# Causal score quarters and a redistributed mask in a gated linear attention kernel with a router

## The chip, the cores and the metric

The kernel runs on one core of one Trainium2 chip. Its time is the device time in microseconds (us) of one execution; the time before is 432.96 us, the median of 3 runs (432.19 to 433.65). The engines are called as in the profile: PE is TensorE (PEld its weight loads), DVE is VectorE, ACT is ScalarE, POOL is GpSimd, SP is SyncE, which only issues transfers. SBUF is the working memory, PSUM the memory that PE writes, in banks of 512 float32 values per partition. All data is float32.

## The reference, cut to what matters

A gated linear attention feeds a mixture of eight experts. For each of 4 batches and 8 heads a state of 48 x 48 decays and grows along 768 time steps; the result is regrouped to 3072 tokens of 384 values, a router picks one expert for each token, and that expert's two layers are run.

```python
# attention, q k v alpha: (4, 8, 768, 48)
for t in range(S):
    state = alpha[:, :, t, :, None] * state + np.einsum('bhd,bhe->bhde', k[:, :, t], v[:, :, t])
    y[:, :, t] = np.einsum('bhd,bhde->bhe', q[:, :, t], state)
# router and experts, x: (3072, 384), E = 8, F = 1024
logits = xn @ en.T / tau            # xn, en: rows over their norms
expert_idx = np.argmax(logits, axis=1)
for e in range(E):
    mask = expert_idx == e
    h = np.maximum(x[mask] @ w1[e], 0.0)
    out[mask] = gate_w[mask, None] * (h @ w2[e])
```

## The kernel before

The sequence of a batch is cut into 6 chunks of 128 steps, so there are NS = 24 chunks, each with 8 heads in NP = 4 pairs; a pair's two heads (hh = 0, 1) lie in partitions 0 to 63 and 64 to 127, 48 of each 64 used. A loop of 27 steps works as a pipeline: step s loads and decays chunk s, forms the scores of chunk s-1, and mixes chunk s-2 into rows. Within a chunk, the output of time i is a sum over times j up to i, so scores above the diagonal are masked.

Decays and scores. `pa`, `pk`, `pq` and `pkb` are transposes by PE into PSUM; they and `px` take turns in three banks.

```python
def decays(s):
    pa = turned(at_s[i], "pa")                      # PE, 4 transposes
    nc.vector.tensor_tensor_scan(r..., pa..., inr...)
    pk = turned(kt_s[i], "pk")
    nc.vector.tensor_tensor(krf, pk, r, ALU.mult)
    pq = turned(qt_s[i], "pq")
    nc.scalar.copy(qc, pq)
def decay_queries(s):
    nc.vector.reciprocal(ini..., rv[:, :, 0:1])
    d["a_scan"] = nc.vector.tensor_tensor_scan(a, pa, ini, 0.0, ALU.mult, ALU.add)
    nc.gpsimd.tensor_tensor(qs, d["qc"], a, ALU.mult)
# keys_back(s): pkb = transposes of kr, nc.scalar.copy(kb, pkb)
def scores(s):
    d["sm"] = sm = [work.tile([P, NP, P], FP32, name=f"sm{hh}") for hh in range(2)]
    sc = [ps_sc.tile([P, NP, P], FP32, name=f"sc{hh}") for hh in range(2)]   # a bank each
    for p in range(NP):
        for hh in range(2):
            sl = slice(DP * hh, DP * hh + DP)
            mm(sc[hh][:, p], lhsT=kr[sl, p], rhs=qs[sl, p], start=True, stop=True)
    nc.vector.tensor_tensor(sm[0], sc[0], causal.to_broadcast([P, NP, P]), ALU.mult)
    nc.scalar.copy(sm[1], sc[1])
    nc.gpsimd.affine_select(out=sm[1], in_=sm[1], pattern=[[0, NP], [1, P]], base=0,
        channel_multiplier=-1, compare_op=ALU.is_ge, fill=0.0)
```

Mixing, rows and routing. `px` holds a chunk's rows and, in 8 further columns per quarter, its logits.

```python
def mix_chunk(s):                     # after mix_states, which adds dec x qs to pyx
    for hh in range(2):
        ... mm(pyx[hh]..., lhsT=vt[:, 2 * p + hh], rhs=sm[hh][:, p], ...)
        nc.scalar.copy(yT[hh]..., pyx[hh][:, 0:YX])          # ycols
def update(s): ...                    # pd = kb x v, then state on DVE
def rows(s):
    ... mm(px[sl, hh, q], lhsT=yT[hh][:, q, sl], rhs=sel[:, hh, q], ...)
    nc.vector.tensor_reduce(x[:, LG : LG + E]..., px[:, :, :, 2 * D :]..., op=ALU.add)
    nc.scalar.copy(x[:, 0:DM]..., px[:, :, :, 0 : 2 * D]...)
def choose(g):                        # DVE: top, win, win, best, chosen; POOL: before
def place(g, total=False):            # PE: rk, two products; DVE:
    nc.vector.tensor_tensor(at, rk, ch, ALU.mult)
    nc.vector.tensor_reduce(row.unsqueeze(2), at, axis=AX.X, op=ALU.add)
    nc.vector.tensor_copy(dest[:, s0:s1], row)
    send.extend(range(s0, s1))
for s in range(NS + 3):
    load(s + 2); keys_back(s - 1); decays(s); decay_queries(s); decay_state(s - 1)
    scores(s - 1)                     # issued after the scan a of step s
    mix_states(s - 2); mix_chunk(s - 2); update(s - 1); rows(s - 2)
    r = s - 3                         # a group whose last row is r is placed here
    ...
    # one placed row is scattered to its expert per step; after row 15: fetch_early(), weights(0)
    # a group whose last row is s - 2 is chosen here
```

The expert phase follows the loop; the change does not touch it.

Of the kernel before, what the change touches and what calls it, by code (L numbers as in the profile page):

```python
# [9 lines left out]
FP32 = mybir.dt.float32  # L10
I32 = mybir.dt.int32
AF = mybir.ActivationFunctionType
ALU = mybir.AluOpType
AX = mybir.AxisListType
# [13 lines left out]
def kernel(  # L28
# [12 lines left out]
    nc = tc.nc  # L41
    B, H, S, D = q.shape
    E, DM = expert_emb.shape
    F = w1.shape[2]
    P = 128
    DP = 64
    NP = H // 2
    NCH = S // P
    N = B * S
    NS = N // P  # L50
# [4 lines left out]
    HALF = P // 2  # L55
# [3 lines left out]
    LG, TK, ROW = DM, DM + E, DM + E + 1  # L59

    GROUPS = (
        (0, 3), (3, 6), (6, 9), (9, 12), (12, 14), (14, 16), (16, 19), (19, 21), (21, 23), (23, 24)
    )
    GMAX = max(b - a for a, b in GROUPS)

    S0, EARLY = 16, 2
# [12 lines left out]
    causal = consts.tile([P, 1, P], FP32)  # L79
# [19 lines left out]
    dest = consts.tile([P, NS], I32)  # L99
# [90 lines left out]
    def mm(*args, **kwargs):  # L190
        last["pe"] = nc.tensor.matmul(*args, **kwargs)  # L191
# [4 lines left out]
    def in_turn():  # L196
        return tc.issue_after(last["pe"].ins) if last else ExitStack()


    with ExitStack() as c1:  # L200
        keep = c1.enter_context(tc.tile_pool(name="keep", bufs=1))
        work = c1.enter_context(tc.tile_pool(name="work", bufs=2))
# [9 lines left out]
        kt_s = [keep.tile([P, H, DP], FP32, name=f"kt{i}") for i in range(NBUF)]  # L212
        vt_s = [keep.tile([P, H, DP], FP32, name=f"vt{i}") for i in range(NBV)]

        NR = 3
        r_s = [keep.tile([P, NP * P], FP32, name=f"r{i}") for i in range(NR)]

# [3 lines left out]
        def fixed_parts():  # L221
            for i in range(NBUF):
                nc.gpsimd.memset(at_s[i][:, :, D:DP], 1.0)

                nc.gpsimd.memset(at_s[i][0:1], 0.0)
                nc.vector.memset(kt_s[i][:, :, D:DP], 0.0)
                nc.vector.memset(qt_s[i][:, :, D:DP], 0.0)
                if i == 0:
                    nc.gpsimd.memset(inr, 0.0)
                    for p in range(NP - 1):  # L230
                        nc.gpsimd.memset(inr[:, p * P + P - 1 : (p + 1) * P], 1.0)
                    for j in range(NR):
                        nc.vector.memset(r_s[j][:, NP * P - 1 :], 1.0)
                if i < 2:
                    nc.vector.memset(ini_s[i], 0.0)
            make_upper_triangular(nc, causal[:, 0], val=1.0, diag=True)
            for i in range(NBV):
                nc.vector.memset(vt_s[i][:, :, D:DP], 0.0)

# [104 lines left out]
        def place(g, total=False):  # L344

            s0, s1 = GROUPS[g]
            n = s1 - s0
            ch = chosen[:, s0:s1]
            bank = ps_mm.tile([P, GMAX + 1, E], FP32, tag="mm", name="rk")
            rk = bank[:, 0:n]  # L350
            rkf = rk.rearrange("p s e -> p (s e)")
            mm(
                rkf, lhsT=ones, rhs=before[:, s0:s1].rearrange("p s e -> p (s e)"),
                start=True, stop=False,
            )
            mm(
                rkf, lhsT=earlier, rhs=ch.rearrange("p s e -> p (s e)"),
                start=False, stop=True,
            )
            if total:  # L360

                mm(bank[:, GMAX], lhsT=ones, rhs=before[:, s1], start=True, stop=True)
            at = work.tile([P, GMAX, E], FP32, name="at_row")[:, 0:n]
            nc.vector.tensor_tensor(at, rk, ch, ALU.mult)
            row = work.tile([P, GMAX], FP32, name="row")[:, 0:n]
            nc.vector.tensor_reduce(row.unsqueeze(2), at, axis=AX.X, op=ALU.add)
            nc.vector.tensor_copy(dest[:, s0:s1], row)
            send.extend(range(s0, s1))
            if not total:
                return None  # L370
            m = work.tile([P, E], FP32, name="n")
            nc.vector.tensor_tensor(m, bank[:, GMAX], ebase, ALU.subtract)
            return m

        def first_expert(n):

            ok = work.tile([P, E], FP32, name="ok")
            nc.vector.scalar_tensor_tensor(
                out=ok, in0=n, scalar=float(EARLY * P), in1=first, op0=ALU.is_ge, op1=ALU.mult
            )  # L380
            lead = work.tile([P, 1], FP32, name="lead")
            nc.vector.tensor_reduce(lead, ok, axis=AX.X, op=ALU.max)
            nc.vector.tensor_scalar(lead, lead, -1.0, float(E), ALU.mult, ALU.add)
            nc.vector.tensor_scalar(turn_f, cols, lead, None, ALU.add)
            wrap = work.tile([P, E], FP32, name="wrap")
            nc.vector.tensor_scalar(wrap, turn_f, float(E), float(E), ALU.is_ge, ALU.mult)
            nc.vector.tensor_tensor(turn_f, turn_f, wrap, ALU.subtract)
            nc.vector.tensor_copy(turn_i, turn_f[0:1])
            r0 = work.tile([1, E], FP32, name="r0")
            nc.vector.tensor_scalar(r0, turn_f[0:1], float(N), None, ALU.mult)  # L390
            nc.vector.tensor_scalar(r0[:, 0:1], r0[:, 0:1], float(EARLY * P), None, ALU.add)
            nc.vector.tensor_copy(row0, r0)
# [67 lines left out]
        def behind(s):  # L460

            queue = ExitStack()
            for call in st[s]["last"]:
                queue.enter_context(tc.issue_after(call.ins))
            return queue
# [94 lines left out]
        def scores(s):  # L560

            d = st[s]
            kr, qs = d["kr"], d["qs"]
            d["sm"] = sm = [work.tile([P, NP, P], FP32, name=f"sm{hh}") for hh in range(2)]
            sc = [ps_sc.tile([P, NP, P], FP32, name=f"sc{hh}") for hh in range(2)]
            for p in range(NP):
                for hh in range(2):
                    sl = slice(DP * hh, DP * hh + DP)
                    mm(
                        sc[hh][:, p], lhsT=kr[sl, p], rhs=qs[sl, p], start=True, stop=True  # L570
                    )
            nc.vector.tensor_tensor(sm[0], sc[0], causal.to_broadcast([P, NP, P]), ALU.mult)
            nc.scalar.copy(sm[1], sc[1])
            nc.gpsimd.affine_select(
                out=sm[1], in_=sm[1], pattern=[[0, NP], [1, P]], base=0,
                channel_multiplier=-1, compare_op=ALU.is_ge, fill=0.0,
            )

        NQ = NP // 2
# [33 lines left out]
        def rows(s):  # L615

            yT = st[s]["yT"]
            px = ps_tr.tile([P, 2, NQ, 2 * D + E], FP32, tag="tr", name="px")
            for hh in range(2):
                for q in range(NQ):  # L620

                    for i in range(2):
                        sl = slice(i * HALF, (i + 1) * HALF)
                        mm(
                            px[sl, hh, q], lhsT=yT[hh][:, q, sl], rhs=sel[:, hh, q],
                            start=True, stop=True, skip_group_check=True,
                        )
            g = group_of[s]
            s0, s1 = GROUPS[g]
            if s == s0:  # L630
                x_g[g] = work.tile([P, GMAX, ROW], FP32, name="x", bufs=4)[:, 0 : s1 - s0]
            x = x_g[g][:, s - s0]
            nc.vector.tensor_reduce(
                x[:, LG : LG + E].unsqueeze(2), px[:, :, :, 2 * D :].rearrange("t a q e -> t e a q"),
                axis=AX.XY, op=ALU.add,
            )
            nc.scalar.copy(
                x[:, 0:DM].rearrange("t (q j a d) -> t a q j d", q=NQ, j=2, a=2),
                px[:, :, :, 0 : 2 * D].rearrange("t a q (j d) -> t a q j d", j=2),
            )  # L640


# [21 lines left out]
        def warm(n):  # L664

            pw = ps_mm.tile([P, P], FP32, tag="mm", name="pw")
            for _ in range(n):
                mm(pw, lhsT=ident, rhs=ident, start=True, stop=True)

        send = []  # L670
        warm(7)
        fixed_parts()
        load(0)
# [3 lines left out]
        for s in range(NS + 3):  # L677
# [58 lines left out]
                with behind(s):  # L736
                    nc.gpsimd.memset(blank, 0.0)

            r = s - 3
            if r >= 0:  # L740
                g = group_of[r]
                if r == GROUPS[g][1] - 1:
                    with in_turn():
                        n = place(g, r in (S0 - 1, NS - 1))
                    if r == S0 - 1:
                        with behind(s):
                            first_expert(n)
            with behind(s) if s < NS else ExitStack():
                for c in send[:] if s >= NS else send[:1]:
                    to_rows(dest[:, c : c + 1], x_g[group_of[c]][:, c - GROUPS[group_of[c]][0]])  # L750
# [6 lines left out]
            r = s - 2  # L757
# [15 lines left out]
    with ExitStack() as c3:  # L773
# [132 lines left out]
        fill = []  # L906
# [343 lines left out]
```

## Time and profile before

| stretch, us | what | PE busy | DVE busy | ACT busy | POOL busy |
|---|---|---|---|---|---|
| 0 to 14.03 | start, steps 0 and 1 | 11.39 | 10.78 | 6.29 | 8.16 |
| 14.03 to 147.38 | steps 2 to 23 of the loop | 128.81 | 109.89 | 62.38 | 87.26 |
| 147.38 to 166.59 | last steps, first expert begun | 19.21 | 6.03 | 6.83 | 8.38 |
| 166.59 to 430.70 | experts | 252.82 | 154.19 | 99.10 | 88.58 |

The span is 430.7 us. Busy times are sums over instructions; the ends of matmuls are modelled, so start-to-start times say more of PE. In lines of the profile, out<-in names the tiles, L is the line of the kernel, an x is the number of instructions in the group, and what stands after <- in brackets is what ended the idle time ahead of the instruction. Mean durations that matter here: ACT's score copy of 512 elements per partition 586 ns, a ycols copy of 256 elements 373 ns, ACT's x copy 484 ns; DVE's mask multiply of 512 elements 667 ns, its scans 1214 and 1222 ns, its kr multiply 691 ns; POOL's select of 512 elements 642 ns.

### The profile page before, as it was taken

How to read it: one execution, taken by the hardware profiler on the slowest of the kernel's cores; microseconds unless marked ns; L12 is line 12 of the kernel's file. 1: busy time of each engine (PE TensorE's matmuls, PEld its weight loads, DVE VectorE, ACT ScalarE, POOL GpSimd, SP SyncE). 2: the span in 40 equal slices, each digit the busy share in tenths (PEclk: the TensorE clock that was granted, in tenths of full speed). 3: DMA queues.
4: the chain of work that ended last, by engine and by line, in shares of the span. 5: the costliest groups of instructions: out<-in, count | busy, mean ns of one | idle time of the engine just before them, and what ended most of it. 6: DMA issues, size and time to landing. Idle time of an engine off the chain costs nothing. (4 is left out here: it accounts for less than half of the span.)

```text
span 430.7 us, 10669 instructions
## 1 busy us (share of the span) xinstructions
PE 412.2 (96%) x3970; PEld 361.2 (84%) x3970; DVE 280.9 (65%) x749; ACT 174.6 (41%) x406; POOL 192.4 (45%) x285
## 2 busy tenths in 40 slices
PE   7999999999989999999999999999999999999995
PEld 6888888888878877779899789798878979978984
DVE  7888778788788614854865856833781684693631
ACT  4444544444444434463532522522261352352410
POOL 7555777667655826911007118023601802702701
PEclk9999999999999999999999999999999999999998
DMA  9999899999957942868108209105602800001001
GB/s 139 158 167 161 179 183 190 192 187 198 185 111 216 389 148 94 260 224 317 66 16 299 101 21 350 38 37 186 200 19 70 320 2 36 21 0 49 4 17 38
DMA packets 119371, 60.15 MB, mean 140 GB/s; under 512 B 102287, under 2 KB 113816, under 8 KB 119312
## 3 DMA queue, kind: packets, MB, share of 16 engines
q1 hardware_dynamic: 115208, 49.14, 50.1%
q0 software_dynamic: 3728, 10.16, 6.7%
q8 instruction: 38, 0.62, 0.7%
q14 instruction: 21, 0.17, 0.1%
q10 hardware_dynamic: 376, 0.05, 0.1%
HBM read 49.69 MB, written 11.45 MB: 142 GB/s over the span
## 5 line engine op out<-in xcount | busy, mean ns | idle before, releaser
L805 POOL DMA_INDIRECT out_dram<-y,sx x25 | 24.3, 972 | 164.4 <-DVE xT_m L964 81.1
L987 PE MATMUL pq<-xT,w 128*128 128x192 f32 x280 | 64.4, 328 | 1.5 <-PEq L1148 0.7
L987 PEld LDWEIGHTS pq<-xT,w 128*128 128x128 f32 x280 | 47.3, 190 | 3.2 <-issue 2.5
L910 DVE TENSOR_TENSOR hT<-pq,v 128x192 f32<-128x192 f32 x84 | 29.9, 356 | 28.3 <-PE pq L987 25.9
L508 POOL TENSOR_TENSOR qs<-qc,a 128x512 f32<-128x512 f32 x24 | 30.7, 1279 | 33.6 <-DVE a L504 24.4
L894 PE MATMUL pyo<-w,hT 128*128 128x384 f32 x128 | 43.3, 492 | 0.0
L987 PE MATMUL pq<-xT_m,w_m 128*128 128x192 f32 x168 | 36.8, 328 | 1.5 <-ACTq L1148 1.2
L894 PEld LDWEIGHTS pyo<-w,hT 128*128 128x128 f32 x128 | 23.7, 190 | 15.3
L995 ACT ACTIVATE hT<-hT 128x384 f32<-128x384 f32 (+1 forms) x56 | 24.8, 443 | 24.9 <-DVE hT L910 20.2
L480 DVE TENSOR_TENSOR_SCAN r<-pa,inr 128x511 f32<-128x511 f32 x24 | 29.1, 1214 | 5.3 <-PE pa L194 5.1
L987 PEld LDWEIGHTS pq<-xT_m,w_m 128*128 128x128 f32 x168 | 28.7, 190 | 2.3 <-ACTq L1148 1.8
L313 POOL DMA_INDIRECT xs<-x,dest x24 | 24.8, 1032 | 11.3 <-DVE best L337 4.5
L504 DVE TENSOR_TENSOR_SCAN a<-pa,ini 128x512 f32<-128x512 f32 x24 | 29.3, 1222 | 0.7
L1035 PE MATMUL pq<-w_m,hT_m 128*128 128x192 f32 x168 | 29.6, 326 | 0.0
L934 POOL TENSOR_TENSOR w_m<-w 128x384 f32<-128x384 f32 x28 | 27.5, 1004 | 4.0 <-DMA out_dram<-y,sx 1.7
L910 DVE TENSOR_TENSOR v<-pq,v 128x192 f32<-128x192 f32 x56 | 20.0, 356 | 12.7 <-ACT v L998 5.6
L995 ACT ACTIVATE hT<-pq 128x192 f32<-128x192 f32 x28 | 9.3, 331 | 46.8 <-PE pq L987 46.8
L191 PE MATMUL sc<-qs,kr 64*128 64x128 f32 x384 | 27.9, 285 | 0.0
L1035 PEld LDWEIGHTS pq<-w_m,hT_m 128*128 128x128 f32 x168 | 27.7, 190 | 0.0
L934 POOL TENSOR_TENSOR w_m<-w,w_m 128x384 f32<-128x384 f32 x28 | 27.1, 996 | 0.0
L191 PEld LDWEIGHTS sc<-qs,kr 64*128 64x128 f32 x384 | 23.3, 187 | 4.0 <-issue 3.0
L191 PE MATMUL pyx<-sm,vt 128*64 128x128 f32 x384 | 26.3, 279 | 0.0
(199 smaller groups left out, 895.0 us busy)
## 6 DMA issues: line engine op xcount, KB each, us to landing
w<-in_moe_w_dram SPq DMA_DIRECT2D x16, 1536.0 KB
kt<-in_k_dram SPq DMA_DIRECT2D x24, 192.0 KB
qt<-in_q_dram SPq DMA_DIRECT2D x24, 192.0 KB
vt<-in_v_dram SPq DMA_DIRECT2D x24, 192.0 KB
xg<-xs SPq DMA_DIRECT2D x22, 196.5 KB
at<-in_alpha_dram SPq DMA_DIRECT2D x24, 168.0 KB
xg<-xs SPq DMA_DIRECT2D x8, 98.2 KB
at<-in_alpha_dram SPq DMA_DIRECT2D x24, 22.5 KB
```

What stands on the lines that cost most here:

```text
L191: last["pe"] = nc.tensor.matmul(*args, **kwargs)
L313: ins = nc.gpsimd.indirect_dma_start(out=xs, out_offset=bass.IndirectOffsetOnAxis(ap=rows, axis=0), in_=x, in_offset=None, bounds_check=E ...
L480: nc.vector.tensor_tensor_scan(r[:, L - 2 :: -1], pa[:, L - 1 : 0 : -1], inr[:, L - 2 :: -1], 1.0, ALU.mult, ALU.add,)
L504: d["a_scan"] = by_dve = nc.vector.tensor_tensor_scan(a, pa, ini, 0.0, ALU.mult, ALU.add)
L508: by_pool = nc.gpsimd.tensor_tensor(qs.rearrange("p n t -> p (n t)"), d["qc"], a, ALU.mult)
L805: ins = nc.gpsimd.indirect_dma_start(out=out, out_offset=bass.IndirectOffsetOnAxis(ap=col, axis=0), in_=y, in_offset=None, bounds_check=N - 1,
L894: pe[:] = [nc.tensor.matmul(py, lhsT=hT[:, f], rhs=w2_t[:, f], start=(f == 0), stop=(f == FT - 1),)]
L910: dve[:] = [call(*args)]
L934: nc.gpsimd.tensor_tensor(to[:, f], x[:, f], y[:, f], ALU.subtract)
L987: pe[:] = [nc.tensor.matmul(to, lhsT=left, rhs=right, start=start, stop=stop, skip_group_check=True,)]
L995: return nc.scalar.activation(h, p, AF.Relu)
L1035: pe[:] = [nc.tensor.matmul(to, lhsT=left[:, f], rhs=right[:, f], start=start and f == 0, stop=stop and f == n - 1, skip_group_check=True,)]
```

## The change

It aims at PE's score products and at DVE. Scores below the diagonal block need only half of a chunk's times: of the keys of the later half only the queries of the later half matter. So each product of 64 x 128 weights and 128 columns becomes two products of 64 keys, the first with 128 columns, the second with 64, laid so that four of them can lie in different quarters of the array; for odd pairs the two halves swap their PSUM partitions and are put right as they are copied out. The mask of odd pairs of the first head moves from DVE to an ACT copy and a POOL select. The logits leave PSUM by ACT, so that the px bank no longer waits for DVE. Ranks are taken one step later for most groups, there are eight routing groups in place of ten, and the rank sum is written as an integer at once. The sm tiles become fixed ones whose never-written quarter is cleared at the start.

```diff
     GROUPS = (
-        (0, 3), (3, 6), (6, 9), (9, 12), (12, 14), (14, 16), (16, 19), (19, 21), (21, 23), (23, 24)
+        (0, 4), (4, 8), (8, 12), (12, 14), (14, 16), (16, 20), (20, 23), (23, 24)
     )
...
+            for t in sm_s[0] + sm_s[1]:
+                nc.vector.memset(t[HALF:P, :, 0:HALF], 0.0)
...
-            row = work.tile([P, GMAX], FP32, name="row")[:, 0:n]
-            nc.vector.tensor_reduce(row.unsqueeze(2), at, axis=AX.X, op=ALU.add)
-            nc.vector.tensor_copy(dest[:, s0:s1], row)
+                nc.vector.tensor_reduce(dest[:, s0:s1].unsqueeze(2), at, axis=AX.X, op=ALU.add)
...
-            d["sm"] = sm = [work.tile([P, NP, P], FP32, name=f"sm{hh}") for hh in range(2)]
+            d["sm"] = sm = [sm_s[hh][s % 2] for hh in range(2)]
...
             for p in range(NP):
-                for hh in range(2):
-                    sl = slice(DP * hh, DP * hh + DP)
-                    mm(
-                        sc[hh][:, p], lhsT=kr[sl, p], rhs=qs[sl, p], start=True, stop=True
+                for half in range(2):
+                    i0, to = half * HALF, (half + p) % 2 * HALF
+                    for hh in range(2):
+                        sl = slice(DP * hh, DP * hh + DP)
+                        mm(
+                            sc[hh][to : to + HALF, p, i0:P],
+                            lhsT=kr[sl, p, i0 : i0 + HALF], rhs=qs[sl, p, i0:P],
+                            start=True, stop=True,
+                            skip_group_check=True,
+                        )
+            for rows_in, rows_out, p, i in (
+                (every, every, 0, hi), (lo, lo, 0, lo), (hi, lo, 1, every), (lo, hi, 1, hi),
+            ):
+                if p == 0:
+                    shp = [rows_in.stop - rows_in.start, NP // 2, i.stop - i.start]
+                    nc.vector.tensor_tensor(
+                        sm[0][rows_out, p::2, i], sc[0][rows_in, p::2, i],
+                        causal[rows_in, :, i].to_broadcast(shp), ALU.mult,
                     )
-            nc.vector.tensor_tensor(sm[0], sc[0], causal.to_broadcast([P, NP, P]), ALU.mult)
-            nc.scalar.copy(sm[1], sc[1])
-            nc.gpsimd.affine_select(
-                out=sm[1], in_=sm[1], pattern=[[0, NP], [1, P]], base=0,
-                channel_multiplier=-1, compare_op=ALU.is_ge, fill=0.0,
-            )
+                else:
+                    nc.scalar.copy(sm[0][rows_out, p::2, i], sc[0][rows_in, p::2, i])
+                nc.scalar.copy(sm[1][rows_out, p::2, i], sc[1][rows_in, p::2, i])
+            for t, n in ((sm[0][:, 1::2], NP // 2), (sm[1], NP)):
+                nc.gpsimd.affine_select(
+                    out=t, in_=t, pattern=[[0, n], [1, P]], base=0,
+                    channel_multiplier=-1, compare_op=ALU.is_ge, fill=0.0,
+                )
...
-            nc.vector.tensor_reduce(
-                x[:, LG : LG + E].unsqueeze(2), px[:, :, :, 2 * D :].rearrange("t a q e -> t e a q"),
-                axis=AX.XY, op=ALU.add,
-            )
+            lg = work.tile([P, 2, NQ, E], FP32, name="lg", bufs=1)
+            nc.scalar.copy(lg, px[:, :, :, 2 * D :])
             nc.scalar.copy(
                 x[:, 0:DM].rearrange("t (q j a d) -> t a q j d", q=NQ, j=2, a=2),
                 px[:, :, :, 0 : 2 * D].rearrange("t a q (j d) -> t a q j d", j=2),
+            )
+            nc.vector.tensor_reduce(
+                x[:, LG : LG + E].unsqueeze(2), lg.rearrange("t a q e -> t e a q"),
+                axis=AX.XY, op=ALU.add,
             )
...
+        placed_at = {}
+        for g, (_, s1) in enumerate(GROUPS):
+            soon = s1 == S0 or s1 > NS - 3
+            placed_at.setdefault(s1 + (2 if soon else 3), []).append(g)
...
-            r = s - 3
-            if r >= 0:
-                g = group_of[r]
-                if r == GROUPS[g][1] - 1:
-                    with in_turn():
-                        n = place(g, r in (S0 - 1, NS - 1))
+            for g in placed_at.get(s, ()):
+                r = GROUPS[g][1] - 1
+                with in_turn():
+                    n = place(g, r in (S0 - 1, NS - 1))
...
```

More of the change, by code (lines that the diff above doesn't have):

```diff
@@ L213 @@
         vt_s = [keep.tile([P, H, DP], FP32, name=f"vt{i}") for i in range(NBV)]
+        sm_s = [[keep.tile([P, NP, P], FP32, name=f"sm{hh}{i}") for i in range(2)] for hh in range(2)]
         NR = 3
@@ L364, in place @@
             nc.vector.tensor_tensor(at, rk, ch, ALU.mult)
-            row = work.tile([P, GMAX], FP32, name="row")[:, 0:n]
-            nc.vector.tensor_reduce(row.unsqueeze(2), at, axis=AX.X, op=ALU.add)
-            nc.vector.tensor_copy(dest[:, s0:s1], row)
+            with nc.allow_low_precision(reason="a whole number and zeros"):
+                nc.vector.tensor_reduce(dest[:, s0:s1].unsqueeze(2), at, axis=AX.X, op=ALU.add)
             send.extend(range(s0, s1))
@@ new lines, in scores @@
+            lo, hi = slice(0, HALF), slice(HALF, P)
+            every = slice(0, P)
+            for rows_in, rows_out, p, i in (
[6 more added lines that the diff above has]
+                        causal[rows_in, :, i].to_broadcast(shp), ALU.mult,
+                    )
+                else:
+                    nc.scalar.copy(sm[0][rows_out, p::2, i], sc[0][rows_in, p::2, i])
+                nc.scalar.copy(sm[1][rows_out, p::2, i], sc[1][rows_in, p::2, i])
@@ L737 @@
                     nc.gpsimd.memset(blank, 0.0)
-            r = s - 3
-            if r >= 0:
-                g = group_of[r]
-                if r == GROUPS[g][1] - 1:
-                    with in_turn():
-                        n = place(g, r in (S0 - 1, NS - 1))
-                    if r == S0 - 1:
-                        with behind(s):
-                            first_expert(n)
+            for g in placed_at.get(s, ()):
+                r = GROUPS[g][1] - 1
+                with in_turn():
+                    n = place(g, r in (S0 - 1, NS - 1))
+                if r == S0 - 1:
+                    with behind(s):
+                        first_expert(n)
             with behind(s) if s < NS else ExitStack():
```

## The prediction

> **What bounds the kernel now.** I read the busy table first, then the waits of TensorE (PE), then the timeline of one step of the attention loop, since the change touches only that loop. By the busy table PE is busy 96% of the span and ScalarE (ACT) 41%: PE is the bound and ACT looks free.
>
> ```profile
> PE 412.2 (96%) x3970; PEld 361.2 (84%) x3970; DVE 280.9 (65%) x749; ACT 174.6 (41%) x406; POOL 192.4 (45%) x285
> ...
> PE pk L194 <- ACT x L637: 1.9, 2, 1.2
> PE rk L191 <- DVE x L633: 1.8, 2, 0.9
> ```
>
> The last two lines are from the view of who waited for whom: the only PE waits of this loop above 0.5 us. The timeline of one plain step gives the rest (columns: start, duration, engine, line, operation, out<-in):
>
> ```profile
> 62.68 0.60 PE L194 MATMUL pa<-ident,at 128*128 128x128 f32 x4
> ...
> 63.31 1.22 DVE L480 TENSOR_TENSOR_SCAN r<-pa,inr 128x511 f32<-128x511 f32 x1 [0.82 <-PE pa L194]
> ...
> 64.16 1.16 PE L191 MATMUL sc<-qs,kr 64*128 64x128 f32 x16
> ...
> 64.64 0.69 DVE L487 TENSOR_TENSOR kr<-pk,r 128x512 f32<-128x512 f32 x1
> ...
> 65.25 0.67 PE L191 MATMUL pyx<-qs,dec 64*64 64x128 f32 x16
> ...
> 65.44 0.59 ACT L573 COPY sm<-sc 128x512 f32<-128x512 f32 x1 [0.54 <-PE sc L191]
> 65.45 1.22 DVE L504 TENSOR_TENSOR_SCAN a<-pa,ini 128x512 f32<-128x512 f32 x1
> ...
> 66.59 0.66 DVE L572 TENSOR_TENSOR sm<-sc,causal 128x512 f32<-128x512 f32 x1
> 66.60 0.81 ACT L613 COPY ycols<-pyx 128x256 f32<-128x256 f32 x2 [0.57 <-PE pyx L191]
> ...
> 67.23 0.89 PE L191 MATMUL px<-sel,ycols 128*64 128x104 f32 x16
> ...
> 68.05 0.66 PE L194 MATMUL pkb<-ident,kr 128*128 128x128 f32 x4
> ...
> 68.54 0.60 PE L194 MATMUL pa<-ident,at 128*128 128x128 f32 x4
> ```
>
> From pa to pa is 68.54 - 62.68 = 5.86 us, and PE's groups follow without a gap (matmul ends are modelled, so I use starts: scores 65.25 - 64.16 = 1.09 us). ACT turns pyx into ycols at once when pyx is done (66.60), because its score copy hangs on PE alone. VectorE (DVE) works from the scan r to the mask multiply sm, 62.68 + 3.91 = 66.59, and nothing on PE needs that multiply before the next step. The 22 steps in which ycols exists as well as a new chunk run from 14.03 to 147.38 in the timeline, 133.35 us.
>
> **What the Trainium skill says.** "PSUM — Partial Sum Buffer", section "PSUM bank collisions raise a hardware error": two engines may not touch one bank and quadrant at once, reads against reads included. The kernel before obeys without cost: DVE reads only score bank sc0, ACT only sc1. The same page, "Engine vs sequencer instructions": "ScalarE/VectorE/GpSimdE queues are strict FIFO." The trace agrees, on DVE: in the step whose pa starts at 85.96, r could start 0.63 later, at 86.59, and starts at 87.12, behind a win from 86.54 that it does not need. "TensorE: Matmul & The Clock Gate", "Part 3: Packing small matmuls — row/col tiling": tiles of the array work at the same time. The trace agrees: eight products of 128 columns take 0.59 us in quarters (65.25 to the next group at 65.84), 1.09 us in halves by rows. "Perfetto Trace Analysis", "Optimizing Scalar/DVE Operations": each instruction carries a fixed overhead; here ACT copies take 586 ns for 512 elements and 373 for 256 (rows sm and ycols), so 160 ns plus 0.83 ns per element.
>
> **The change part by part.** All estimates are lines through such rows.
>
> Scores on PE: 8 products become 16 quarter products, half with 128 and half with 64 columns, 75% of the columns. Two bounds: 0.59 us x 2 x 0.75 = 0.89 us by the quartered group; 32 passes x 37 ns (0.59/16) = 1.19 us if each pass costs the same. I take 0.95, saving 0.14 per step, if PE still sets the step.
>
> Masks: DVE multiplies 2 x 128 elements in place of 512. Rows of 667 ns (512) and 420 (state, 256) give about 0.29 us each; an instruction starts some 0.08 us before the end of the one ahead (sm at 66.59, a ending 66.67), so both end 0.50 after the start, at pa + 4.41 in place of pa + 4.57. ACT gets six copies (2 of 256, 4 of 128: 2 x 373 + 4 x 267 = 1.81 us) for one of 586, and a logits copy of about 190 ns: 4.4 us of ACT per step. GpSimd gets one more select, about 0.4 us. Neither is full in 5.86 us.
>
> What decides is a wait. In the changed program ACT's two copies from sc0 wait for DVE's second multiply of the same step (they share the bank), and in ACT's queue ycols stands behind them, mostly with one sc1 copy between. DVE's multiplies still stand behind scan a. px needs ycols, pkb and the next pa stand behind px on PE, and the next r needs that pa. So a ring closes that did not exist before: pa -> r -> kr -> a -> multiplies -> ACT sc0 copies -> ycols -> px -> pkb -> pa. Its length, from pa: multiplies end 4.41; +0.04 to ACT (the delay from DVE's x to ACT's x at 62.49 to 62.53); three copies start to start 0.29 + 0.19 + 0.19; ycols0 starts 5.12, ends 5.49; +0.06 to px, whose halves take 0.41 each (the second needs ycols1, done 5.79, in time); px ends 6.37; pkb 0.49 (68.05 to 68.54): next pa at about 6.85. That is 0.98 above 5.86. The PE saving lies inside the new idle time and is worth nothing.
>
> Sum over the 22 steps. In 7 of them (around a batch's last chunk) pkb does not stand between px and pa: ring 6.35. So 15 x 6.84 + 7 x 6.35 = 147.1. Choosing a group's experts is DVE work that now lies on the ring: before, such a step had its multiply 0.66 later (86.33 top, multiply at 90.53, pa 85.96); with DVE now fed through ACT's copy I take 0.8 for each of four groups of 4 rows and 0.57 for two of 2 rows: 4.3. First expert's small operations, one of which now stands between the two multiplies (turn_f, 870 ns): 1.3. Constants in one step 0.2. Rank products (0.44 per group before) on PE between px and pa: 2.9. Total 155.8 against 133.35: +22.4 us.
>
> What the change gives is already in this sum: the waits of rk (about 2.6 us over all groups, by the gaps ahead of rk) and of pk on ACT's x (2.2) vanish, since px now leaves its bank by ACT alone and ranks come a step later; two groups fewer spare 0.9 of PE; reduction straight into integers spares DVE about 0.25 each. They were worth near 6 us of PE-bound time and now lie in PE's idle time. Later row scatters start the first weight load two steps later, after the row-15 scatter of step 22: some 6 us remain from issue to use, and loads ran at 250 to 400 GB/s; I add 0.5 at most. Start, tail (scores not behind a scan) and experts are unchanged. 432.96 + 22.4 = 455.4.
>
> **Rivals.** (1) PE stays the bound: then 24 x 0.14 + 4.8 + 0.9 = 9 us less, 424 us. For it: PE 96% against ACT's 41%. Against: averages don't show a ring, and its DVE part alone is 3.8 us, with 2.4 of ACT and PE after it. (2) The quarter products are bound by passes, 1.19 us: +2.4, less the vanished waits, 430. Speaks for it: 37 ns per pass in quarters; but it too needs PE to be the bound. (3) Ring plus more: DVE's small operations between two SBUF operands run at times far over their mean beside GpSimd (turn_f 870 ns, win 522); on the ring each counts, 465 us. (4) The wait on DVE is usually over when ACT gets there: only if the multiplies came ahead of a, which the program order excludes.
>
> **Range and chances.** The ring rests on measured rows, and every link is in the program; its length may be off by 0.3 us, so 22 x 0.3 = 6.6, and the additions by half: 446 to 465. Half the excess would still exceed 2% (8.7 us), so slower over 2% has 0.91, within 2% 0.05, faster 0.04.
>
> **What would show it.** After: steps of about 6.85 us from pa to pa; PE idle ahead of px, ended by ACT ycols, about 1 us each; ACT's sm copy idle ahead of it, ended by DVE's sm; PE's busy share in the loop down to some 85%; no PE wait of pk on ACT x. Wrong if px follows pd without a gap, or ycols starts before DVE's multiplies end.

## The result, and the profile after

The changed kernel takes 468.13 us, the median of 4 runs (467.26 to 470.26), beside 433.30 for the kernel before on the same chip: a ratio of 1.0814, 95% interval 1.077 to 1.0858. I had predicted 455.4, with 446 to 465 as the range. So the direction was as told, and the size was 12.7 us short; that the mechanism was as told too is what the profile and experiments 1 and 9 show below. The profiled execution is the longest of the four (470.26, a span of 468.1), 2.1 us above the median, which matters below.

The busy table, the row of the granted clock, and the costliest group with a wait, of the kernel after (the last column is idle time of PE ahead of these instructions, and who ended it):

```profile
PE 412.6 (88%) x4346; PEld 360.5 (77%) x4346; DVE 273.5 (58%) x753; ACT 198.9 (42%) x550; POOL 200.2 (43%) x307
...
PEclk9999899998999997999999999999999999999998
...
L191 PE MATMUL px<-sel,ycols 128*64 128x104 f32 x384 | 24.4, 274 | 33.4 <-ACT ycols L637 33.4
```

PE is about as busy as before in sum (412.6 against 412.2 us), but its share falls from 96% to 88%: the time was added as idle time, not as work. (The sum hides two things: shorter products, and some work at a lower clock, both below.) No other engine is near full. The view of waits names the pair (waited for: total us, times, longest):

```profile
PE px L191 <- ACT ycols L637: 33.4, 22, 2.8
PE phe L191 <- DMA w<-in_moe_w_dram: 4.4, 1, 4.4
...
PE pk L194 <- ACT x L660: 0.6, 2, 0.3
...
ACT sm L595 <- DVE sm L590: 26.0, 22, 2.3
```

The first and the last line are the two links that the change added, both 22 times, once in each step. The waits of before, pk for x and rk for x, have shrunk to 0.6 or gone. The second line, the first expert's weights, had no part in the waits of before.

The timeline of one step shows the ring whole (columns: start, duration, engine, line, operation):

```profile
120.40 0.60 PE L194 MATMUL pa<-ident,at 128*128 128x128 f32 x4
...
121.25 1.21 DVE L483 TENSOR_TENSOR_SCAN r<-pa,inr 128x511 f32<-128x511 f32 x1
...
122.57 0.69 DVE L490 TENSOR_TENSOR kr<-pk,r 128x512 f32<-128x512 f32 x1
...
123.38 1.22 DVE L507 TENSOR_TENSOR_SCAN a<-pa,ini 128x512 f32<-128x512 f32 x1
...
124.52 0.45 DVE L590 TENSOR_TENSOR sm<-sc,causal 128x128 f32<-128x128 f32 x2
...
125.01 0.64 ACT L595 COPY sm<-sc 64x256 f32<-64x256 f32 x2 [1.32 <-DVE sm L590]
125.55 0.26 ACT L596 COPY sm<-sc 64x128 f32<-64x128 f32 x1
125.83 0.65 ACT L637 COPY ycols<-pyx 128x256 f32<-128x256 f32 x2
...
126.26 0.93 PE L191 MATMUL px<-sel,ycols 128*64 128x104 f32 x16 [1.61 <-ACT ycols L637]
127.12 0.66 PE L194 MATMUL pkb<-ident,kr 128*128 128x128 f32 x4
...
127.61 0.60 PE L194 MATMUL pa<-ident,at 128*128 128x128 f32 x4
```

Read it from top to bottom: each line starts when the one above lets it. ACT stands idle 1.32 us until DVE's multiplies end, PE 1.61 until ycols. The step is 127.61 - 120.40 = 7.21, of which 0.2 is a choice's DVE work ahead of r; a plain step is 7.01 (28.38 to 35.39).

By stretches, from the table by windows of the kernel after (length, then busy time of PE, PEld, DVE, ACT, POOL, granted clock, DMA share, GB/s):

```profile
14.08:177.98 163.90, 128.74 (x2365) 111.57 (x2363) 101.68 (x235) 85.43 (x264) 93.65 (x170) 0.97 0.75 129
177.98:203.62 25.64, 21.21 (x194) 16.89 (x194) 5.67 (x40) 7.92 (x24) 9.68 (x14) 0.87 0.83 292
```

Against before: the loop +30.55 (133.35), the tail +6.43 (19.21), the experts, 203.62 to 468.10, +0.37 (264.11). I had the loop at 155.8 and the tail unchanged but for 0.5. So two places are open: 8.1 us in the loop and 6 in the tail. In the tail the wait for weights shows at once. In the loop, three steps stand out with 8.53, 9.24 and 9.05 us, and there the clock was low:

```profile
46.00:48.50 2.50, 0.31 (x3) 0.07 (x1) 1.72 (x5) 0.71 (x3) 2.20 (x5) 1.00 0.92 120
48.80:50.40 1.60, 1.56 (x16) 1.33 (x16) 0.00 (x0) 0.75 (x2) 0.76 (x4) 0.52 1.19 201
50.40:53.00 2.60, 2.60 (x24) 2.41 (x26) 1.52 (x3) 0.63 (x3) 0.12 (x1) 0.64 1.18 143
```

The first row has PE at work for 0.31 us in 2.5; in the next two it works at 0.52 and 0.64 of its clock: px takes 1.59 us from start to start there and 0.87 elsewhere. The Trainium skill, "TensorE: Matmul & The Clock Gate", "Part 1: The HAM clock gate", tells of half the clock after at least one idle window of about 3.4 us; here a wait of 2.53 us was enough, which is shorter than the page has it.

### The profile page after: what moved, and what is told of

The parts are those of the page before. It is cut to its first block, busy times and chain, and to the rows that moved or that the text cites. A ratio compares the mean times of both kernels' runs of the same rounds, so it can differ in the third digit from the quotient of the medians.

```text
span 468.1 us, 11617 instructions
## 1 busy us (share of the span) xinstructions
PE 412.6 (88%) x4346; PEld 360.5 (77%) x4346; DVE 273.5 (58%) x753; ACT 198.9 (42%) x550; POOL 200.2 (43%) x307
## 5 line engine op out<-in xcount | busy, mean ns | idle before, releaser
L191 PE MATMUL px<-sel,ycols 128*64 128x104 f32 x384 | 24.4, 274 | 33.4 <-ACT ycols L637 33.4
L191 PEld LDWEIGHTS px<-sel,ycols 128*64 128x64 f32 x384 | 19.2, 146 | 37.4 <-ACT ycols L637 36.7
L664 DVE TENSOR_REDUCE x<-lg 128x8 f32<-128x32 f32 x24 | 5.0, 207 | 45.9 <-ACT lg L659 43.8
L596 ACT COPY sm<-sc 128x128 f32<-128x128 f32 (+1 forms) x96 | 25.1, 287 | 10.4 <-PE sc L191 6.9
## 6 DMA issues: line engine op xcount, KB each, us to landing
at<-in_alpha_dram SPq DMA_DIRECT2D x24, 22.5 KB
```

Of the source, the lines that this page charges most:

```text
L596: nc.scalar.copy(sm[1][rows_out, p::2, i], sc[1][rows_in, p::2, i])
```

## The experiments

No experiment leaves out a part of the computation; where one repeats work, it is said. Each ratio is to the kernel before, run beside it on the same chip; medians of different groups of runs can differ by some 0.3%, as the kernel before took 431.83 to 433.30 in them.

**1. Theory and rival.** Theory: the ring through the bank that DVE and ACT share sets the loop, the late weights the tail. Rival: ACT, with six copies more per step, or the quarter products are simply too much. First, undo only the order: ACT's two copies from sc0, and the select behind them, go behind the step's ycols copies.

```diff
-                    nc.scalar.copy(sm[0][rows_out, p::2, i], sc[0][rows_in, p::2, i])
+                    late.append((sm[0][rows_out, p::2, i], sc[0][rows_in, p::2, i]))
...
                     mix_chunk(s - 2)
+            if 0 <= s - 1 < NS:
+                with tc.issue_after(st[s - 2]["ycols"].ins) if s >= 2 else ExitStack():
+                    scores_late(s - 1)      # these copies, and the select of sm[0]
```

> The changed kernel with one thing moved: ACT's two copies out of bank sc0 (and the GpSimd select on them) come after the step's two ycols copies in ACT's queue. Same instructions, same loads on every engine. Ring theory: ycols no longer waits for DVE's multiplies, PE sets the step again; its groups in the changed kernel's timeline sum to 0.44+0.44+0.56+0.72+0.55+0.93+0.46+0.87+0.49 = 5.46 us, so the loop shrinks from 163.9 to about 120 us; the wait for the first expert's weights stays or grows (4.4 to 8 us with the clock it costs): 427 us, between 420 and 433. Rival, too much work: if the time is lost because ACT and GpSimd have more instructions or the quarter products are dear, nothing changes: 464 to 470.

Measured (this version is called e1_ycols_first further down): 437.09 us, ratio 1.0108 (1.0084 to 1.0133). The same instructions, 31 us less. A plain step of its timeline:

```profile
63.97 0.65 ACT L645 COPY ycols<-pyx 128x256 f32<-128x256 f32 x2
...
64.82 0.45 DVE L591 TENSOR_TENSOR sm<-sc,causal 128x128 f32<-128x128 f32 x2
...
65.36 0.64 ACT L608 COPY sm<-sc 64x256 f32<-64x256 f32 x2 [0.74 <-DVE sm L591]
...
65.78 0.60 PE L194 MATMUL pa<-ident,at 128*128 128x128 f32 x4
```

ycols now starts ahead of DVE's multiplies, ACT still waits for them afterwards, and it harms nothing: the pa of this step started at 60.39, so it took 5.39 us. So the rival (464 to 470) falls. The 427, and the range to 433, are missed too: the loop is 127.95 us (14.67 to 142.62) and not 120. PE works for 121.43 of it and idles for the rest: steps with a choice do not shrink to 5.4 (one takes 7.48, from 42.05 to 49.53, behind an operation "chosen" of 1.27 us at 41.20 that holds up DVE's second multiply). The tail holds the other loss, which the expectation had allowed for:

```profile
PE phe L191 <- DMA w<-in_moe_w_dram: 7.0, 1, 7.0
```

With a shorter loop the wait for weights grows from 4.4 to 7.0 us.

**2. The weights alone.** In the changed kernel row 15 is scattered in step 22 and not in step 20, and the weights of the first expert are asked for behind it. Here they are asked for at the end of step 21, the ring stays.

```diff
                     if c == S0 - 1:
                         fetch_early()
-                        weights(0)
+            if s == NS - 3:
+                weights(0)
```

> The changed kernel with the first expert's weights asked for in step 21 in place of after row 15's scatter (step 22). Theory of the tail: the 4.4 us wait of PE for these weights goes, and with it the half clock after it (2 us): 461 to 463. Rival: the weights come no earlier because transfers are full, or PE waits for the early rows instead: 467 to 469.

Measured: 460.66, ratio 1.0656 (1.0632 to 1.068), just under the expected range: 7.5 us less than the changed kernel by the medians, 6.8 by the ratios (1.58% of 433), more than the wait of 4.4. The tail by windows:

```profile
175.96:194.91 18.95, 18.95 (x194) 15.39 (x194) 5.67 (x40) 7.93 (x24) 9.70 (x14) 1.00 0.62 219
```

25.64 us at a clock of 0.87 became 18.95 at 1.00, 6.7 us less: the wait of 4.4, and about 2.3 of work at the low clock behind it.

**3. Both.**

> Both edits together. Ring theory and tail theory together: 120 us of loop, no weight wait: 418 to 424, faster than the kernel before. If the loop was lost to the amount of work: 461 to 463.

Measured: 427.79, ratio 0.9894 (0.9875 to 0.9913). The two cures add up and now the kernel beats the one before, by 1.1%, which is less than expected (418 to 424). The profiled execution is the longest of five (430.91, the other four 427.44 to 427.83). In it PE's work in the loop fell to 121.34 us, and the loop is 130.03. The longest wait in it is new:

```profile
PE pxe L194 <- DMA xg<-xs: 2.9, 1, 2.9
```

It is for the early tokens, whose last row still goes in step 22. That the four shorter executions have this wait in full is not shown; it is about as long as their distance from the profiled one.

**4. The quarter products alone**, in the kernel before: VectorE masks all of sc0 in four pieces, ACT copies sc1 in four; no copy of ACT's reads sc0, so there is no ring.

```diff
-            nc.vector.tensor_tensor(sm[0], sc[0], causal.to_broadcast([P, NP, P]), ALU.mult)
-            nc.scalar.copy(sm[1], sc[1])
+            for rows_in, rows_out, p, i in (...):          # the four pieces
+                nc.vector.tensor_tensor(sm[0][rows_out, p::2, i], sc[0][rows_in, p::2, i], ...)
+                nc.scalar.copy(sm[1][rows_out, p::2, i], sc[1][rows_in, p::2, i])
```

> The kernel before with only the quarter products: DVE masks all of sc0 in four pieces, ACT copies all of sc1 in four, no bank is shared by DVE and ACT, groups and logits as before. Ring theory: without the shared bank no ring; the products take 0.72 in place of 1.09 us and the following group 0.05 less, so 24 x 0.4 = 10 us less, 423, up to 428 if DVE's extra 0.4 us per step lengthens its waits. Rival, dear quarters or too many ACT copies: 433 or more.

Measured: 436.97, ratio 1.0106 (1.0081 to 1.013), a miss; the number is the rival's, but the quarters are not dear: the products take 0.72 us in most steps, 0.37 less than before, and plain steps are 5.4 to 5.6. Yet the loop is 138.15 in the profiled execution (the longest of four, 439.82). Its waits:

```profile
PE rk L191 <- DVE x L651: 6.7, 6, 1.2
PE pk L194 <- ACT x L655: 4.3, 7, 1.9
PE pd L191 <- DMA vt<-in_v_dram: 3.0, 1, 3.0
```

A shorter PE step brings the ranks to PE before DVE has their logits (1.8 us before, 6.7 now), and pk waits 4.3 us for ACT's x in place of 1.9. The third wait came once, and is about as long as this execution is above the median. The first two are what the later ranks and ACT's logits are for: it fits that the parts of the change need each other. But DVE also does more here (119.24 us in the loop, 109.89 before), and in experiment 6 that alone brings such waits; the two causes were not separated.

**5 and 6. More time on VectorE, with the ring and without.** The masking multiplies are issued twice, with the same values, in the changed kernel and in the one before.

```diff
-                    nc.vector.tensor_tensor(sm[0]..., sc[0]..., causal..., ALU.mult)
+                    for _ in range(2):
+                        nc.vector.tensor_tensor(sm[0]..., sc[0]..., causal..., ALU.mult)
```

> The changed kernel with each of VectorE's two masking multiplies issued twice (the second writes the same values), nothing else. Theory (a ring decays -> multiply -> ScalarE's copies of the same bank -> ycols -> px -> pkb -> decays sets the step): the two multiplies took 0.45 us a step together, so each of 22 steps grows by 0.45: 468.1 + 9.9 = 478 us (475 to 481). Rival (VectorE's multiplies lie beside other work, and the step is long for the clock or for GpSimd): 467 to 470 us.

> The kernel before with its one masking multiply (0.58 us) issued twice, nothing else: the same load on VectorE, 0.58 us a step and 12.8 in all, where no ring is closed, as ScalarE reads another bank and TensorE is the bound. Ring theory: 432 to 437 us, since VectorE has 23 us to spare in the loop. Rival (any time more on VectorE moves the step, with or without the ring): 442 to 446 us.

Measured: 476.41 with the ring (ratio 1.1014, 1.0985 to 1.1043), 8.3 us more than the changed kernel and in the expected range (475 to 481); 440.89 without (1.0179, 1.0162 to 1.0196), 8.1 more than before, between the two ranges that I gave. Taken as sums, the two don't differ, and the test doesn't tell the theories apart. By steps they do. Without the ring a plain step is 5.87 (58.21 to 64.08), the 5.86 of before, so the double multiply costs nothing there; the loop's 8.2 us more (141.59 for 133.35) come in other steps, where ranks are taken:

```profile
PE rk L191 <- POOL xg L735: 4.1, 4, 1.4
PE pk L194 <- ACT x L638: 3.5, 4, 2.4
PE rk L191 <- DVE x L634: 2.3, 3, 1.1
```

These three are 9.9 us, against 3.7 for rk and pk before. With the ring, the loop grew from 163.90 to 172.43, but this sum can't be read as the ring alone: the granted clock in the loop was 0.92, against 0.97 in the changed kernel, and in three steps the order on ACT had turned and ycols came first (px waited only 0.2 there). One step that has neither, at a clock of 1.00 in both profiles, is 6.51 in the changed kernel (35.39 to 41.90) and 7.06 here (37.38 to 44.44): 0.55 more, for multiplies that take 1.10 in place of 0.45. So in a plain step more time on VectorE moves the step where the ring is closed, and does not where it is open.

**7. The clock.** Five dummy products stand ahead of px in the changed kernel, in PE's idle time.

```diff
             px = ps_tr.tile([P, 2, NQ, 2 * D + E], FP32, tag="tr", name="px")
+            if s < NS - 2:
+                for _ in range(5):
+                    mm(px.rearrange("p a q e -> p (a q e)")[:, 0:P], lhsT=ident, rhs=ident, ...)
```

> The changed kernel with five dummy products of 128 columns ahead of px in every step, in the time in which TensorE waits for ycols; they write part of px's own bank and are overwritten. Theory (three steps of 8.5 to 9.2 us are long because the granted clock fell to 0.52 to 0.74 after the longest waits): the dummies shorten the wait that TensorE sees from 1.5 to about 0.5 us, the clock stays at 1.0, these three steps return to 7.1 us: 463 to 465 us. Rival (the long steps come from VectorE and GpSimd, the clock only follows): 467 to 472 us.

Measured: 464.68 (1.0739, 1.071 to 1.0768), in the range, with a loop of 160.77 at a clock of 1.00. That looks like the theory's 3 us, but experiment 2 had its loop at 160.86 without any dummy. So I put the two together.

**8. The clock and the weights.**

> The changed kernel with the five dummy products ahead of px and with the weights asked for at the end of step 21: both losses that the prediction had no term for are taken out, only the ring is left. Theory (the two are separate and add): 468.1 - 3.5 - 7.5 = 457 us (455 to 459), of which the ring, 22 steps of 7.03 in place of 6.84, explains the 4 us over or under the predicted 455.4 less the 2 us of tail clock. Rival (the two overlap, as the dummies already shortened the wait for weights to 3.2): 459 to 462 us.

Measured: 461.30 (1.0664, 1.0647 to 1.068): the rival's range, nothing gained on experiment 2 (460.66). Its loop:

```profile
13.49:174.78 161.29, 152.39 (x2585) 133.20 (x2583) 101.55 (x236) 85.25 (x264) 93.82 (x170) 1.00 0.81 154
```

The three long steps are 7.81, 7.84 and 8.06 here, 8.26, 8.37 and 8.04 in experiment 2; that is 1.0 us for the clock, and the step after the first of them, at a clock of 0.85 there, is 8.04 in place of 7.58. The dummies take 1.31 us a step and delay px where the wait was shorter, which gives as much back. So I estimate the clock in the loop at 1 to 1.5 us in the execution of experiment 2, and at some 3 in the profiled, longest execution of the changed kernel (8.53 + 9.24 + 9.05 less these three is 3.1). In that of experiment 2, a wait of 2.87 us left the clock alone:

```profile
109.56 0.94 PE L191 MATMUL px<-sel,ycols 128*64 128x104 f32 x16 [2.87 <-ACT ycols L637]
```

The next group, pkb, starts at 110.42, so px is 0.86 from start to start, and the clock in the whole next step (110.91 to 118.37) is 1.00. Which waits of 2 to 3 us lower the clock differs even within one execution: in the changed kernel's, px took 1.56 us after a wait of 2.03 at 79.45, and 0.93 after one of 2.03 at 169.64. Why its profile had three such places and that of experiment 2 two was not settled.

**9. The ring cut at the bank.** Weights early; VectorE masks all four pieces of sc0, ACT reads sc1 alone, ACT's order is left.

```diff
-                if p == 0:
-                    nc.vector.tensor_tensor(sm[0]..., sc[0]..., causal[rows_in, :, i]..., ALU.mult)
-                else:
-                    nc.scalar.copy(sm[0][rows_out, p::2, i], sc[0][rows_in, p::2, i])
+                nc.vector.tensor_tensor(sm[0]..., sc[0]..., causal[rows_out, :, i]..., ALU.mult)
```

> The changed kernel with weights asked for at the end of step 21, in which VectorE masks all four pieces of bank sc0 (two multiplies more), so that ScalarE reads only sc1, by four copies in place of six, and GpSimd's second select goes; the order in ScalarE's queue is left as it was. It cuts the ring at the shared bank, where e1_ycols_first cut it at the order of the queue. Theory (the wait of ScalarE for VectorE in one bank closes the ring): steps of 5.4 to 5.6 us, 428 to 433 us; the longer VectorE may bring waits in the steps with a choice. Rival (ScalarE has too many small copies in a step, whatever they wait for): the four sc1 copies and the logits copy remain, so 445 to 452 us.

Measured: 431.80, ratio 0.9991 (0.9974 to 1.0007), in the theory's range. Both cuts work, at the queue's order and at the bank:

```profile
63.47 0.65 ACT L634 COPY ycols<-pyx 128x256 f32<-128x256 f32 x2
...
64.21 1.19 DVE L589 TENSOR_TENSOR sm<-sc,causal 128x128 f32<-128x128 f32 x4
...
65.28 0.60 PE L194 MATMUL pa<-ident,at 128*128 128x128 f32 x4
```

DVE's masks take 1.19 us instead of 0.45 and end at 65.40, after the next pa, yet the step is 5.40 (59.88 to 65.28), because nothing of ACT's waits for them. This agrees with the Trainium skill, "PSUM — Partial Sum Buffer", "PSUM bank collisions raise a hardware error", by which two engines have to be kept apart in one bank and quadrant of the partitions: the wait belonged to the sharing. That it was not ACT's load is shown by experiment 1, which keeps all six copies; here there are four. The two engines also shared the tile sm0 that they write, and this cut ends that too; but writing apart in one tile needed no wait elsewhere in the changed kernel (DVE wrote its part of x from 127.78, during ACT's copy into x, 127.72 to 128.20).

**10 to 12. What the quarters are worth.** First, the changed kernel with the scores and masks of before and the weights early.

> The changed kernel with the scores and masks of the kernel before (full products, one multiply, one copy, one select), and the first expert's weights asked for at the end of step 21: what the later ranks, ScalarE's logits, the eight groups and the shorter rank chain give alone. Theory (the waits of rank products for x, and of pk for x, go, and the rank products get fewer, as the prediction worked out): 426 to 429 us. Rival (the waits come back elsewhere, at the early rows that are fetched later, or at pk): 430 to 434 us.

Measured: ratio 0.9892 (0.987 to 0.9914), and 428.58 us, the median of four runs (427.53 to 431.08), where a fifth, of 434.12 at a lower granted clock, is left out; in the theory's range. Then, here and in the version of experiment 3, two finished rows are scattered per step from step 17 on, to bring the early tokens sooner:

```diff
-                for c in send[:] if s >= NS else send[:1]:
+                for c in send[:] if s >= NS else send[: 2 if s > S0 else 1]:
```

> The same early scatter on the version that keeps the full scores and masks of the kernel before and has only the other parts of the change, with the weights asked for early. Theory: the wait of 2.8 us for the early tokens goes here too, 429.3 - 3 to 5 = 424 to 426 us, and the quarter scores are worth only the difference to the version with them, 1 to 3 us and not 24 x 0.37 = 8.9, as the shorter TensorE step is eaten by its waits. Rival (quarters are worth what they save on TensorE): this one at 425 and the one with quarters at 418 or less.

> The version with both ends of the ring and of the weights opened (ycols ahead of ScalarE's copies of sc0, weights asked for at the end of step 21), and from step 17 on two finished rows scattered in a step in place of one, so that row 15 goes in step 19 and not 22. Theory (the 2.9 us that TensorE waited there for the early tokens, and the clock lost after it, go): 427.8 - 2.9 - 1 to 2 = 423 to 424 us (421.5 to 425.5). Rival (GpSimd's second scatter in a step delays its multiply of queries, or the fetch collides with the loads): 427 to 430 us.

Measured: 427.67 without quarters (0.9885, 0.987 to 0.99), 430.38 with them (0.9942, 0.9928 to 0.9955). Both are above their theory's range. The latter is slower than experiment 3 and just above its rival's range; its 423 had taken the wait of 2.9 us, read in the longest execution, off a median of shorter ones. The two loops, without quarters and then with:

```profile
14.03:141.42 127.39, 126.69 (x2010) 112.09 (x2011) 106.70 (x213) 65.38 (x151) 84.90 (x146) 1.00 1.06 195
```

```profile
14.03:143.14 129.11, 122.69 (x2362) 106.92 (x2363) 102.19 (x236) 86.59 (x263) 92.26 (x168) 1.00 1.00 192
```

Without quarters PE idles 0.70 us in the whole loop: it is the bound, and the loop can only shrink with its work. With quarters it works 4.0 us less and idles 6.4, most of it ended by ACT's x, lg and ycols. A step with a choice shows how the gain is eaten: this one of 7.49 us (41.74 to 49.23) has the operation "chosen" between DVE's two multiplies at 1.28 us beside POOL's qs, and r of the next step, the copies of ACT and the bank for pq follow late. Whether the scatter itself cost time on POOL I did not separate. So three versions beat the kernel before by some 1.1%: the rest of the change without quarters (0.9892, and 0.9885 with the rows sooner), and quarters with ycols first (0.9894). In the best versions of either kind the quarters are worth nothing that these runs can tell.

## Why the prediction was wrong in size

- **The ring, its links and its place on the path: right.** Experiments 1 and 9 cut it in two places, and the step falls from 7.0 to 5.4 both times. The signs came as named: idle ahead of px ended by ACT's ycols, idle ahead of ACT's sm ended by DVE's sm. Two sizes were off: PE idles 33.4/22 = 1.5 us per step and not about 1, and its busy share in the loop is 79% (128.74/163.90) and not some 85%, since the step is longer and the products are shorter than I took them.
- **The step that failed first, on the later weight load: "I add 0.5 at most".** I compared the time to the first use, some 6 us, with the time of the load at a rate of 250 to 400 GB/s, 3.9 to 6.3 us for its 1536 KB. The first load was issued at 174.66 in the timeline and PE could start at 184.09, 9.4 us later; PE was there at 179.66, after 5.0, and waited 4.4. The rate was hardly what was wrong: 260 GB/s on average from 174.66 to 184.09, at the lower end of mine. But that is 2.45 MB in all, and the load is 1.57: other transfers went with it (the expert's second matrix was asked for 0.57 us later). And PE worked on at a lower clock behind the wait, 0.50 from 184.00 to 187.00. Experiment 2 gives the whole term, 6.7 us in the tail. The two ends of the wait, in the timeline of the kernel after:

```profile
174.66 0.38 SPq L141 DMA_DIRECT2D w<-in_moe_w_dram  x1
...
184.09 2.90 PE L191 MATMUL phe<-exT,w 128*128 128x256 f32 x6 [4.43 <-DMA w<-in_moe_w_dram]
```

- **The second: the ring's length, "ycols0 starts 5.12", 6.84 in all.** The multiplies ended almost as added up, at pa + 4.37 once the 0.2 of the choice is taken off (4.41 predicted), and the delays to ACT (0.04) and from ycols to px (0.43) were exact. The three ACT copies ahead of ycols took 0.82 from start to start (125.01 to 125.83) where I had 0.67, and px 0.86 for 0.82: 0.19 more, less the 0.04 of the multiplies. The copies themselves were as taken, 0.37, 0.26 and 0.26 us, but I had each start 0.08 ahead of the end of the one before, and together they gained only 0.07. So a plain step is 7.01 for 6.84, and 0.17 in 22 steps is 3.7 us. The loops of experiments 2 and 8, 160.86 and 161.29, are 5.1 and 5.5 over the 155.8; the ring's length is 3.7 of that.
- **The sum.** 455.4 + 6.2 (6.7 less the 0.5 allowed) + 5.1 (the loop of experiment 2) = 466.7, against 468.1; the 1.4 left is less than the 3.0 by which the four executions differ.
- **What had no term: the clock.** I said nothing of PE's clock after its new idle times. In the loop this is an estimated 1 to 1.5 us of the 5.1, more in some executions; in the tail about 2.3 of the 6.7.
- **Additions for choices, ranks and constants (8.7 in all)** were not measured one by one. With the ring and the clock corrected the loop adds up to 155.8 + 3.7 + 1 to 1.5 = 160.5 to 161.0, against 160.86; that this leaves no room for a large error in them is an argument, no measurement.
- **"The PE saving lies inside the new idle time": right**, and larger than said: 0.72 us for the 0.95 that I took, 0.37 saved per step and not 0.14. Both of my bounds, 0.89 by columns and 1.19 by passes, were too high.
- **Waits of rk and pk vanish: right** (0.6 left for pk). "Worth near 6 us" for these parts where PE is the bound: without quarters, and with the weights early, they bring 4.2 (428.58 for 432.81), and 5.1 with the rows sooner (427.67 for 432.77).
- **Rivals.** The first two needed PE as the bound and fell. The third, DVE's small operations at many times their mean beside POOL, appeared: "chosen" took 1.26 us at 46.26 between the two multiplies, beside qs from 46.22, and the step became 8.53, of it 0.7 by the clock (7.81 in experiment 8, with the same slow operation). In the three other choices of four rows it took about 0.18. The fourth does not occur in the changed kernel: 22 of 22 waits stayed.

## What to carry to other kernels

When work is moved to an engine with idle time, follow what stands behind it in that engine's queue: here two small copies that wait for another engine, placed ahead of the copy that the bound engine needs, cost 31 us, and placing them behind it gave the 31 us back. A load whose start hangs on the pace of a loop must be followed from its issue to its use, with all that is in flight beside it: the rate alone said 3.9 to 6.3 us, and it took 9.4. And 0.37 us saved per step on the bound engine is only a gain when the next wait is more than that away: here waits in other steps took it back.

## What the runs showed that I had not expected

A step's score products in quarters, 32 records in the trace, take 0.72 us, 22.5 ns each, where the 16 records of eight quarter products of 128 columns had taken 0.59, 37 ns each. ACT's three copies from 64 partitions, one of 256 elements and two of 128, take 0.37 and twice 0.26 us and follow each other at 0.27 on average: three small copies in a row cost nearly the sum of their durations, 0.82 of 0.89. The clock fell to 0.52 after a wait of 2.53 us, but stayed at 1.00 after one of 2.87 in another execution.
